# P1 of the second layer by a second Strassen level, the next batch's scores in the fixed banks, w_out in column halves, and fills into open banks

## The chip, the cores and the metric

The kernel runs on one core of a Trainium2 chip. The metric is the device time of one execution in microseconds (us). Five engines work side by side, each through its own queue in order: TensorE (PE), VectorE (DVE), ScalarE (ACT), GpSimd (POOL) and SyncE (SP), which issues the transfers.

## The reference

Two stages follow each other. In the first, x (8 batches, 8 heads, 512 rows, 64 columns) and a state (8, 8, 32, 64) attend to each other in both directions. In the second, the result, 8 x 544 rows of 512, goes through a layer with elu between two weight matrices of 512 x 2048 and 2048 x 512.

```python
def _attn_ref(x, state):
    scale = 1.0 / np.sqrt(D)
    a = softmax(scale * x @ state.T)          # max subtracted, sum + 1e-9
    xread = a @ state                          # 512 rows per batch and head
    a2 = softmax(scale * state @ x.T)
    sread = a2 @ x                             # 32 rows per batch and head
    return concatenate([xread, sread], axis=2)

def _moe_ref(x, w_in, w_out):
    h = x @ w_in
    g = np.where(h > 0, h, np.exp(np.minimum(h, 0)) - 1)
    return g @ w_out
```

(The softmax is abbreviated here.) All is in float32.

## The kernel before

**The order.** A planner in the kernel (`Plan`) records every operation with its engine, a cost and what it reads and writes, then orders them by a list schedule: PE takes its operations in the order of the code as far as they are ready, the other engines take the one that is due first. The kernel emits that order, so all recorded operations carry one line, 450. Banks of PSUM are handed out by the planner too: eight, of which two, numbers 6 and 7 (`fixed`), are kept for the third accumulator of the first layer's chunks once the steady state begins, and six rotate among everything else. Operations that only keep PE busy during the first 40 us (`fill`, line 1485) are put in where PE would idle and a bank is free.

**The stages.** `start()` loads the weights in blocks of 1 MB, converts them with ACT and DVE (16 blocks: the first eight are w_in, stored again to DRAM, the others w_out), and does the first layer of batches 0 and 1 without Strassen. It then does the second layer of batch 0 by one Strassen level, seven products P1 to P7 of 256 x 1024 by 1024 x 256 (`Strassen`). `ffn2(o, 1, x1)` does the rest of batch 1, and builds the second-level weights on the way (`Second.weights`). `batch(b)` for 2 to 7 is the steady state, and `states()` at the end does the 256 rows of the state reads.

**One batch of the steady state.** The first layer is four chunks (`ffn1_chunk`), each a Strassen level of seven products with two calls 128x256. They multiply the softmaxed scores `aT` by `m`, the product of the states and w_in (`make_m`, from w_half fetched back from DRAM). The elu of each quarter is done by ACT and DVE. The second layer (`ffn2`) starts with P1: sixteen calls 128x256 into one bank, copied out twice by ACT. P2, P6, P7, P5, P4 and P3 follow, each by a second Strassen level (`Second`): `sums` makes four sums on DVE, and `steps` has seven steps of four calls 128x128 into two banks in turn. Each step's result is added into `o` by DVE or, where it is the first one there, copied by ACT.

**What is woven into it.** After P1 the next batch's `scores` are taken into two of the rotating banks, and `first_m` makes the first block of m. The softmax of these scores (`softmax`, `softmax_rows`, on DVE, POOL and ACT) stands before P6's steps, with the loads of x (`load_x`), the state transposes with 16 small transfers (`move_state`) and the sums of aT on POOL (`sum_a`). `state_read` comes among P4's steps. The two stores of the batch and the 16 block loads for the batch after (`load_blocks`, into `o`) go through SP's queue.

```python
if six:
    o.sum_1()
    x1 = o.open()
    o.product(x1, o.a11, b11, True)
    A.copy(out=c12, in_=x1)
    A.copy(out=c11, in_=x1)
    second[2].sums(o.a12, s_2[1], a_sb[:, :1024])
    if nxt:
        scores(b + 1, xr)
        first_m(b + 1)
    for f in second[2].steps(c11):
        f()
```

Of the kernel before, what the change touches and what calls it, by code (L numbers as in the profile page):

```python
# [78 lines left out]
class Op:  # L79
    __slots__ = (  # L80
        "number", "engine", "cost", "emit", "deps", "opens", "closes", "port", "moved", "start",
        "end", "due", "users", "name", "instr", "shape", "rank", "rate", "turn", "nudge",
# [3 lines left out]
class Plan:  # L86
# [51 lines left out]
    def add(self, engine, cost, emit, ins, outs, port=False, moved=0, tokens=((), ()), name="", shape=None):  # L138
        op = Op()
        op.number, op.engine, op.cost, op.emit = len(self.ops), engine, cost, emit  # L140
        op.deps, op.opens, op.closes, op.port, op.moved = set(), None, [], port, moved
        op.name, op.shape, op.rank, op.rate = name, shape, None, 350e3
        op.nudge = 0.0
        pieces = []
        banks = {}
        for writes, aps in ((False, ins), (True, outs)):
            for a in aps:
                if isinstance(a, View):
                    banks[id(a.bank)] = a.bank
                else:  # L150
                    pieces.append((writes,) + self.region(a))
        for writes, names in enumerate(tokens):
            for t in names:
                self.writers.setdefault(t, [])
                self.readers.setdefault(t, [])
                pieces.append((bool(writes), t, 1))
        for writes, key, mask in pieces:
            if key is None:
                continue
            for m, o in self.writers[key]:  # L160
                if m & mask:
                    op.deps.add(o)
            if writes:
                for m, o in self.readers[key]:
                    if m & mask:
                        op.deps.add(o)
        for writes, key, mask in pieces:
            if key is None:
                continue
            if writes:  # L170
                self.writers[key] = [
                    (m & ~mask, o) for m, o in self.writers[key] if m & ~mask
                ] + [(mask, op)]
                self.readers[key] = [(m & ~mask, o) for m, o in self.readers[key] if m & ~mask]
            else:
                self.readers[key].append((mask, op))
        for b in banks.values():
            if b.last is None:
                b.first = op
            else:  # L180
                op.deps.add(b.last)
            b.last = op
        op.deps.discard(op)
        self.ops.append(op)
        return op
# [51 lines left out]
    def run(self, until=0.0):  # L237
# [13 lines left out]
        port, wire, shape = 0.0, 0.0, None  # L251
# [4 lines left out]
        def bank_time(op):  # L256
# [4 lines left out]
            if op is not openers[oldest]:  # L261
                need += self.KEPT_BANKS
# [3 lines left out]
        def choice(op):  # L266
            if op.number < self.all_banks:
                return banks
            return [b for b in banks if b[1] not in fixed]

        def pick(e):
# [4 lines left out]
            while able[e] or coming[e]:  # L276
# [4 lines left out]
                for _, n, op in able[e]:  # L281
                    start = max(at, ready[op])
                    if op.port:
                        start = max(start, port)
                    if op in self.opening or op in self.kept:
# [17 lines left out]
        while len(done) < len(self.ops):  # L303
# [8 lines left out]
            if e == PE:  # L312
                t = free_at[PE]
                while at < until and t + 0.5 < at:
                    free = [i for u, i in banks if u <= t]
                    if free:
                        fills.append((t, free[-1]))
# [12 lines left out]
            while oldest < len(openers) and openers[oldest] in opened:  # L330
                oldest += 1
            if e == PE and op.shape != shape:
# [46 lines left out]
def kernel(  # L379
# [49 lines left out]
    ident = pool.tile([P, P], FP32, name="ident")  # L429
    w_out = buffer([FO, DM], "w_out")  # L430
    t_w_sb = buffer([3, FO // 2, 256], "t_w")
    sec = buffer([9728], "sec")
    sec_2 = buffer([1536], "sec_2")
    g_sb = buffer([FO, S], "g")
    kT = buffer([B + 2, P], "kT")
# [5 lines left out]
    soft = buffer([1024], "soft")  # L441
    s_buf = buffer([2048], "s")
    xe = buffer([2048], "xe")
    small = buffer([68], "small")

    make_identity(nc, ident)

    def issue(engine, name, kw):
        def emit():
            ins = getattr(engine, name)(**{k: resolve(v) for k, v in kw.items()})  # L450
# [7 lines left out]
    class Engine:  # L458
# [3 lines left out]
        def __getattr__(self, name):  # L462
            def call(**kw):
# [11 lines left out]
                elif self.key == ACT:  # L475
                    cost = 0.055 + 0.84 * n
                    cost += 0.1 * sum(is_ap(kw[k]) for k in ("scale", "bias") if k in kw)
# [45 lines left out]
    def turn_calls(outs, in_):  # L523
# [28 lines left out]
    def tops(g):  # L552
        return dict(
            top=small[:, g : g + 1], total=small[:, 2 + g : 3 + g],
            top_t=small[:, 4 + 16 * g : 20 + 16 * g], total_t=small[:, 36 + 16 * g : 52 + 16 * g],
        )
# [84 lines left out]
    def scores(b, xT):  # L641
        st[b, "s"] = ps = [bank(), bank()]
# [10 lines left out]
    def make_m(b, *hcs):  # L653
# [10 lines left out]
        products(0.46 * len(hcs), calls, "make_m", "state")  # L664

# [39 lines left out]
    def soft_t(g):  # L705
        return soft[:, g * 512 : (g + 1) * 512]
# [5 lines left out]
    def read(b):  # L712
        return kT[:, B + b if b < 2 else b - 1]

    def softmax_rows(b):
        s = st[b, "s"]
        top, total = small[:, 0:2], small[:, 2:4]
        for g in range(G):
            V.reduce_max(out=tops(g)["top"], in_=s[g], axis=AX_X)
        V.tensor_scalar(out=top, in0=top, scalar1=-scale, scalar2=None, op0=ALU.mult)  # L720
        for g in range(G):
            A.activation(
                out=soft_a(b, g), in_=s[g], func=AF.Exp, scale=scale, bias=tops(g)["top"],
                accum_out=tops(g)["total"],
# [4 lines left out]
    def softmax(b, to):  # L729
        s = st[b, "s"]  # L730
        total_t = small[:, 36:68]

        def rows(g):
            return soft_t(g).rearrange("p (k n) -> p k n", n=NS)

        for g in range(G):
            V.transpose(out=soft_t(g), in_=s[g])
        for g in range(G):
            V.reduce_max(out=tops(g)["top_t"], in_=rows(g), axis=AX_X)
            Q.tensor_tensor(  # L740
                out=rows(g), in0=rows(g), in1=bc(tops(g)["top_t"], NS), op=ALU.subtract
            )
            A.activation(out=soft_t(g), in_=soft_t(g), func=AF.Exp, scale=scale)
            V.reduce_sum(out=tops(g)["total_t"], in_=rows(g), axis=AX_X)
        V.tensor_scalar(out=total_t, in0=total_t, scalar1=eps, scalar2=None, op0=ALU.add)
        V.reciprocal(out=total_t, in_=total_t)
        for g in range(G):
            Q.tensor_tensor(
                out=rows(g), in0=rows(g), in1=bc(tops(g)["total_t"], NS), op=ALU.mult
            )  # L750
            V.transpose(out=to[:, g * 512 : (g + 1) * 512], in_=soft_t(g))
# [23 lines left out]
    def state_read(b, at=x_halves):  # L775
# [12 lines left out]
        for g in range(G):  # L788
            A.activation(
                out=read(b)[:, g * D : (g + 1) * D], in_=ps[:, g * D : (g + 1) * D], func=AF.Copy,  # L790
                scale=tops(g)["total"],
# [52 lines left out]
    def ffn1_chunk(b, c, g_to):  # L844
# [14 lines left out]
        def part_1():  # L859
# [6 lines left out]
            elu(pa, g_to[:, k0, lo], e[0], V)  # L866
# [3 lines left out]
        def part_2():  # L870
# [6 lines left out]
            elu(pc, g_to[:, k0, hi], e[3], V)  # L877
# [10 lines left out]
    w_k = w_out.rearrange("p (k e) (h q) -> p k e h q", e=2, h=2)  # L888
    b11, b12, b21, b22 = (halves(w_k[:, :, e, h]) for e in range(2) for h in range(2))
# [8 lines left out]
    class Second:  # L898
# [23 lines left out]
        def sums(self, a, s, s34=None):  # L922
# [5 lines left out]
            s = s.rearrange("p (i k q) -> p i k q", i=2, q=P)  # L928
            s1, s2 = s[:, 0], s[:, 1]
            if s34 is None:  # L930
                s3, s4 = a21, a12
            else:
                s34 = s34.rearrange("p (i k q) -> p i k q", i=2, q=P)
                s3, s4 = s34[:, 0], s34[:, 1]
# [4 lines left out]
            if s34 is not None:  # L939
                V.tensor_tensor(out=s4, in0=a12, in1=s2, op=ALU.subtract)  # L940
            self.late = s34 is None

        def steps(self, out, fresh=False):
# [6 lines left out]
            def step(n, ps, a, b, first, last, h, c):  # L950
# [11 lines left out]
                o = out[:, h, c * P : (c + 1) * P]  # L962
                if fresh and n in (0, 2, 3, 6):
                    A.copy(out=o, in_=ps)
                else:
                    V.tensor_tensor(out=o, in0=o, in1=ps, op=ALU.add)
# [18 lines left out]
    second[2] = Second(sec_2)  # L985
    s_2 = [sec[:, 7680 + i * 1024 : 7680 + (i + 1) * 1024] for i in range(2)]
# [83 lines left out]
    def weight_block(n, parts=1):  # L1070

        out = []
        for i in range(parts):
# [5 lines left out]
            else:  # L1079
# [3 lines left out]
                dst = w_out[:, rows, q * 256 : (q + 1) * 256]  # L1083
# [6 lines left out]
    def ident_ready(i):  # L1090
        v = fixed[i].view()
# [4 lines left out]
                (v[:, k * P : (k + 1) * P], ident, ident, dict(start=k == 0, stop=True))  # L1096
# [6 lines left out]
    def start():  # L1103
# [79 lines left out]
        late = plan.ops[-1]  # L1183
        n0 = Strassen(2, g0, [m_sb[:, i, :1024] for i in range(2)], s_buf)
# [51 lines left out]
    def ffn2(o, b, x1=None):  # L1236
# [4 lines left out]
        if six:  # L1241
            o.sum_1()
            x1 = o.open()
            o.product(x1, o.a11, b11, True)
            A.copy(out=c12, in_=x1)
            A.copy(out=c11, in_=x1)
            second[2].sums(o.a12, s_2[1], a_sb[:, :1024])
            if nxt:
                scores(b + 1, xr)
                first_m(b + 1)  # L1250
            for f in second[2].steps(c11):
                f()
            second[6].sums(o.s, s_2[0], m_sb[:, 1, :1024])
            combine(o.a12, o.a12, o.s)
            if nxt:
                softmax(b + 1, a_sb)
                softmax_rows(b + 1)
                load_x(b + 1, x_halves)
                move_state(b + 1)
                sum_a()  # L1260
            steps = second[6].steps(c12)
            second[7].sums(o.a21, s_2[1])
            for f in steps:
                f()
            combine(o.s, o.s, o.a11, ALU.add)
            A.copy(out=c21, in_=c12)
        else:
# [3 lines left out]
            second[6].sums(o.s, s_2[0], m_sb[:, 1, :1024])  # L1271
# [10 lines left out]
        if not nxt:  # L1282
            turn_read()
        elif not six:
# [25 lines left out]
        if not six:  # L1310
            second[2].weights(b21)
        for f in second[3].steps(c12):
            f()
        store(b, 0, o)

    def turn_read():
# [3 lines left out]
        for b in range(B):  # L1320
            calls += turn_calls(
                [v[t][:, b] for t in range(2)], read(b)
# [9 lines left out]
    def batch(b):  # L1332
        for hc in range(4, 7):
            fetch(hc)
        if b + 1 < B:
            load_blocks(b + 1, ob)
        p = [None] * FC
# [24 lines left out]
    def state_chunk(c, right):  # L1362
# [15 lines left out]
        spare = (soft, a_sb)[c % 2]  # L1378
# [104 lines left out]
    def fill(i):  # L1483
        tc.keep_in_program_order(
            nc.tensor.matmul(
                psum[:, i, :P], ident, ident, start=True, stop=True, skip_group_check=True
# [4 lines left out]
    for op in steps:  # L1491
        while fills and fills[0][0] <= op.start:
            fill(fills.pop(0)[1])
# [32 lines left out]
```

## Time and profile before

| what | value |
|---|---|
| median of 3 runs | 710.66 us (710.53 to 711.33) |
| the profiled execution | 709.55 us, its span 707.8 us |
| PE busy | 694.1 us, 98% |
| DVE busy | 561.3 us, 79% |
| ACT busy | 292.5 us, 41% |
| POOL busy | 123.5 us, 17% |
| one batch of the steady state | about 76.4 us (250.75 to 327.07, and so on) |
| mean granted PE clock | 0.995 |

The span is the time from the first to the last instruction; the execution's own time has some 1.75 us more around it. Busy time is the union of an engine's instructions. A call of a float32 matmul shows as two records, whose durations overlap those of their neighbours. The chain of waits is followed back from the last instruction: at each step to what released it. In the timeline a line shows start, length, engine, operation and, in brackets, the idle time before it and what ended it. In the table by stretches the columns are the length of the stretch, then busy time and instructions of PE, its weight loads, DVE, ACT and POOL, the granted clock, the share of the transfer engines and GB/s.

### The profile page before, as it was taken

To read this page: it belongs to the slowest core of one execution; us is meant where nothing else is said; L and a number is where in the kernel's file an instruction comes from. 1 tells how busy PE (TensorE), PEld (TensorE's weight loads), DVE (VectorE), ACT (ScalarE), POOL (GpSimd) and SP (SyncE) were. 2 spreads that over 40 slices of the span, in tenths; PEclk is the share of its full clock that TensorE was granted. 3 is DMA by queue.
4 is the path that set the end of the run, shared out by engine and by line. 5 is a ranking of instruction groups with operands and counts; after the bars stand their busy time and mean duration, and the time that the engine had idled before them with its cause. 6 is when DMAs were issued, how large, how long until landed. Compare 5 with 4: busy or idle time off the path is not lost.

```text
span 707.8 us, 14536 instructions
## 1 busy us (share of the span) xinstructions
PE 694.1 (98%) x5792; PEld 592.0 (84%) x5792; DVE 561.3 (79%) x1049; ACT 292.5 (41%) x575; POOL 123.5 (17%) x158
## 2 busy tenths in 40 slices
PE   8799999999999999999999999999999999999997
PEld 7444467889988999889978998899988998999996
DVE  3988999999749984899569974998589955998650
ACT  3979972011147312741075214721284107410530
POOL 1300000023111232120430241123212033000000
PEclk9999999999999999999999999999999999999999
DMA  9578774223263424442373316242444223200300
GB/s 219 185 235 279 253 242 77 61 42 108 61 146 109 116 80 117 123 119 36 99 195 65 86 60 159 96 117 79 125 115 121 49 100 122 61 1 31 119 8 24
DMA packets 132772, 78.55 MB, mean 111 GB/s; under 512 B 113760, under 2 KB 114272, under 8 KB 132704
## 3 DMA queue, kind: packets, MB, share of 16 engines
q1 hardware_dynamic: 130492, 77.06, 39.1%
q8 instruction: 46, 0.75, 0.4%
q10 hardware_dynamic: 2212, 0.56, 0.4%
q14 instruction: 22, 0.18, 0.1%
HBM read 61.34 MB, written 13.11 MB: 105 GB/s over the span
## 4 chain that ended last, share of the span: by engine, by line
PE 94%; ACT 2%; DVE 2%; DMA 1%; issue 0%; POOL 0%; ACTq 0%; DVEq 0%
PE ps L450 93%; DMA xe<-in_x_dram 1%; ACT o L450 1%; DVE w_out L450 1%; ACT w_half L450 0%; ACT t_w L450 0%; DVE s L450 0%; ACT sec L450 0%; POOL soft L450 0%; DVE t_w L450 0%; ACT soft L450 0%; ACTq L450 0%; ACT s L450 0%; DVE g L450 0%; DVE soft L450 0%
## 5 line engine op out<-in xcount | busy, mean ns | idle before, releaser
L450 PE MATMUL ps<-aT,m 128*128 128x256 f32 (+1 forms) x568 | 149.4, 409 | 0.3 <-ACT m L450 0.3
L450 PE MATMUL ps<-w_out,g 128*128 128x128 f32 (+1 forms) x864 | 143.2, 314 | 0.0
L450 PEld LDWEIGHTS ps<-w_out,g 128*128 128x128 f32 x864 | 126.3, 191 | 10.4 <-issue 2.1
L450 PEld LDWEIGHTS ps<-aT,m 128*128 128x128 f32 x568 | 106.1, 191 | 33.1 <-issue 15.2
L450 DVE TENSOR_TENSOR o<-o,ps 128x128 f32<-128x128 f32 (+2 forms) x263 | 73.7, 288 | 53.1 <-PE ps L450 52.4
L450 POOL TENSOR_TENSOR m<-m 128x256 f32<-128x256 f32 x72 | 54.5, 774 | 245.7 <-ACT m L450 244.7
L450 PE MATMUL ps<-sec 128*128 128x128 f32 x560 | 74.7, 276 | 1.8 <-ACT o L450 1.8
L450 PEld LDWEIGHTS ps<-sec 128*128 128x128 f32 x560 | 68.1, 192 | 3.2 <-ACT o L450 2.7
L450 ACT COPY o<-ps 128x128 f32<-128x128 f32 (+2 forms) x54 | 20.5, 406 | 111.8 <-PE ps L450 102.5
L450 PE MATMUL ps<-t_w,s 128*128 128x128 f32 (+1 forms) x432 | 66.1, 300 | 0.0
L450 PEld LDWEIGHTS ps<-t_w,s 128*128 128x128 f32 x432 | 58.9, 191 | 5.7 <-DVE o L450 2.1
L450 ACT ACTIVATE xe<-ps 128x512 f32<-128x512 f32 x96 | 53.6, 600 | 14.1 <-DVE ps L450 8.7
L450 POOL TENSOR_TENSOR soft<-soft,small 128x512 f32<-128x512 f32 x32 | 33.4, 1063 | 147.3 <-DVE small L450 147.3
L450 ACT COPY ps<-ps 128x512 f32<-128x512 f32 (+1 forms) x28 | 15.2, 544 | 102.3 <-PE ps L450 102.0
L450 ACT COPY m<-ps 128x512 f32<-128x512 f32 (+1 forms) x56 | 27.4, 542 | 65.2 <-PE ps L450 65.2
L450 DVE TENSOR_TENSOR ps<-sec,ps 128x512 f32<-128x512 f32 x48 | 32.6, 689 | 15.0 <-PE ps L450 11.8
L450 PE MATMUL ps<-aT,s 128*128 128x256 f32 x168 | 41.0, 379 | 0.0
L450 PE MATMUL ps<-w_half,kT 64*32 64x256 f32 x1024 | 36.1, 389 | 1.9 <-DVE w_half L450 1.9
L450 ACT COPY sec<-ps 128x512 f32<-128x512 f32 x48 | 28.3, 589 | 20.5 <-PE ps L450 20.5
L450 PEld LDWEIGHTS ps<-aT,s 128*128 128x128 f32 x168 | 31.9, 190 | 4.3
L450 DVE TENSOR_TENSOR g<-g 128x512 f32<-128x512 f32 (+1 forms) x37 | 32.9, 890 | 0.1
L450 DVE TENSOR_TENSOR g<-xe,ps 128x512 f32<-128x512 f32 x48 | 32.3, 685 | 0.8
(145 smaller groups left out, 1134.5 us busy)
## 6 DMA issues: line engine op xcount, KB each, us to landing
w_half<-w_in_mem SPq DMA_DIRECT2D x54, 512.0 KB
t_w<-in_moe_w_out_dram SPq DMA_DIRECT2D x8, 1024.0 KB
t_w<-in_moe_w_in_dram SPq DMA_DIRECT2D x7, 1024.0 KB
out_dram<-o SPq DMA_DIRECT2D x14, 512.0 KB
xe<-in_x_dram SPq DMA_DIRECT2D x26, 256.0 KB
o<-in_x_dram SPq DMA_DIRECT2D x80, 64.0 KB
w_in_mem<-w_half SPq DMA_DIRECT2D x8, 512.0 KB
xr<-xr SPq DMA_DIRECT2D x96, 32.0 KB
```

The costliest lines, as they stand in the source:

```text
L450: ins = getattr(engine, name)(**{k: resolve(v) for k, v in kw.items()})
```

## The change

P1 of batches 2 to 7 becomes a second-level product like the other six: a new `second[1]` with its own weights (`sec_1`), its four sums, and seven steps of four calls into c12. The two 128x512 copies fall away; P2's first additions read c12 and write c11 (`base`). After P1's first step stands `first_m`, then the scores, which now go into the two fixed banks. The softmax and what hangs on it stand behind P7's sums. To make room in SBUF, the early softmax buffer, the identity and the small values of batches 0 and 1 move into `sec_1` before its weights are made, and the later softmax works in `xr`. A second identity is made on POOL for the last batch, where `turn_read` comes earlier.

w_out is stored as two column halves, each contiguous, instead of rows of 512. Three of the elus of each batch (of chunk 2 one, of chunk 3 two) take their second pass on ACT instead of DVE. In the planner POOL waits when an operation of DVE [...] would be due first (`give_way`). Where no bank is free, a fill goes into a bank that is open, adding zeros into columns not yet used (`spare`).

```diff
-    w_out = buffer([FO, DM], "w_out")
+    w_out = buffer([2, FO, DM // 2], "w_out")
+    sec_1 = buffer([1536], "sec_1")
...
+        def give_way(op, start):
+            waits = [
+                max(free_at[DVE], t) for t, _, o in coming[DVE] if o.port and o.due < op.due
+            ]
...
+            first = min(waits, default=math.inf)
+            return start if first > start + op.cost else max(start, first + 0.01)
...
                     if free:
-                        fills.append((t, free[-1]))
+                        fills.append((t, free[-1], 0))
+                    elif spare:
+                        fills.append((t, spare.index, 1))
...
-    def scores(b, xT):
-        st[b, "s"] = ps = [bank(), bank()]
+    def scores(b, xT, at=None):
+        st[b, "s"] = ps = at or [bank(), bank()]
...
-            elu(pa, g_to[:, k0, lo], e[0], V)
+            elu(pa, g_to[:, k0, lo], e[0], A if c == 3 else V)
...
-            elu(pc, g_to[:, k0, hi], e[3], V)
+            elu(pc, g_to[:, k0, hi], e[3], A if c > 1 else V)
...
-                o = out[:, h, c * P : (c + 1) * P]
-                if fresh and n in (0, 2, 3, 6):
+                o, p = (x[:, h, c * P : (c + 1) * P] for x in (out, base or out))
+                if n not in (0, 2, 3, 6):
+                    p = o
+                elif fresh:
+                    p = None
+                if p is None:
                     A.copy(out=o, in_=ps)
                 else:
-                    V.tensor_tensor(out=o, in0=o, in1=ps, op=ALU.add)
+                    V.tensor_tensor(out=o, in0=p, in1=ps, op=ALU.add)
...
         if six:
             o.sum_1()
-            x1 = o.open()
-            o.product(x1, o.a11, b11, True)
-            A.copy(out=c12, in_=x1)
-            A.copy(out=c11, in_=x1)
-            second[2].sums(o.a12, s_2[1], a_sb[:, :1024])
+            second[1].sums(o.a11, spaces(m_sb[:, 1], 3) + s_2[0][:1])
+            steps = second[1].steps(c12, fresh=True)
+            steps[0]()
             if nxt:
-                scores(b + 1, xr)
                 first_m(b + 1)
-            for f in second[2].steps(c11):
+                scores(b + 1, xr, [f.view() for f in fixed])
+            else:
+                turn_read()
+            for f in steps[1:]:
                 f()
-            second[6].sums(o.s, s_2[0], m_sb[:, 1, :1024])
+            second[2].sums(o.a12, s_2[1] + spaces(a_sb))
+            for f in second[2].steps(c11, base=c12):
+                f()
+            second[6].sums(o.s, s_2[0] + spaces(m_sb[:, 1]))
             combine(o.a12, o.a12, o.s)
-            if nxt:
-                softmax(b + 1, a_sb)
...
             second[7].sums(o.a21, s_2[1])
+            late = plan.ops[-1]
             for f in steps:
                 f()
             combine(o.s, o.s, o.a11, ALU.add)
             A.copy(out=c21, in_=c12)
+            if nxt:
+                with plan.behind(late):
+                    softmax(b + 1, a_sb)
+                    softmax_rows(b + 1)
+                    load_x(b + 1, x_halves)
+                    move_state(b + 1)
+                    sum_a()
...
             second[2].weights(b21)
+            second[1].weights(b11)
...
+    def fill(i, part):
+        rhs = zeros.to_broadcast([P, P]) if part else ident
         tc.keep_in_program_order(
             nc.tensor.matmul(
-                psum[:, i, :P], ident, ident, start=True, stop=True, skip_group_check=True
+                psum[:, i, part * 256 : part * 256 + P], ident, rhs, start=not part, stop=True,
+                skip_group_check=True,
             )
         )
```

## The prediction

> **What bounds the kernel now.** I read the page's busy shares first, then its chain of waits, then both in time.
>
> ```profile
> PE 694.1 (98%) x5792; PEld 592.0 (84%) x5792; DVE 561.3 (79%) x1049; ACT 292.5 (41%) x575; POOL 123.5 (17%) x158
> ...
> PE 94%; ACT 2%; DVE 2%; DMA 1%; issue 0%; POOL 0%; ACTq 0%; DVEq 0%
> ```
>
> TensorE (PE) is busy for 98% of the span and is 94% of the chain that ended last. The chain in order of time says where the other 6% lie: before 35 us, between 99 and 109 us (VectorE converting the last of w_out), at the end, and five times some 0.33 us on ACT and in handovers, one per batch from 2 to 6. Between them PE runs 76 us without a break:
>
> ```profile
> 34.97 64.67 PE ps L450 x400
> ...
> 251.08 76.00 PE ps L450 x688
> ```
>
> So in the steady state a change is worth what it takes from, or adds to, PE's own queue, plus any new wait. How long a product occupies PE must be read from start to start in PE's timeline, because the listed durations overlap:
>
> ```profile
> 275.96 1.89 PE L450 MATMUL ps<-aT,m 128*128 128x256 f32 x8
> 277.78 1.09 PE L450 MATMUL ps<-w_half,kT 64*32 64x256 f32 x32
> 278.80 8.90 PE L450 MATMUL ps<-aT,m 128*128 128x256 f32 x40
> ...
> 304.30 5.34 PE L450 MATMUL ps<-w_out,g 128*128 128x256 f32 x24
> 309.58 1.09 PE L450 MATMUL ps<-xr,kT 64*32 64x512 f32 x16
> 310.46 1.07 PE L450 MATMUL ps<-w_half,kT 64*32 64x256 f32 x32
> 311.46 2.05 PE L450 MATMUL ps<-w_out,g 128*128 128x128 f32 x16
> 313.35 1.06 PE L450 MATMUL ps<-t_w,s 128*128 128x128 f32 x8
> 314.24 1.06 PE L450 MATMUL ps<-sec,sec 128*128 128x128 f32 x8
> ...
> 326.00 1.06 PE L450 MATMUL ps<-sec 128*128 128x128 f32 x8
> 327.41 1.16 PE L450 MATMUL ps<-sec 128*128 128x128 f32 x8 [0.35 <-ACT o L450]
> ```
>
> One call is two records. 313.35 to 314.24 is 0.893 us for four calls 128 wide, so 0.2233 us a call. Eight records 256 wide take 1.73 us (300.85 to 302.58 in the same answer), so 0.4325 us a call. A call of half the width costs 0.516 of the whole, not 0.5. The last line is the 0.35 us wait: two steps in a row into one bank, the second waiting until ScalarE (ACT) has copied the first out.
>
> The start shows a second limit, in the clock column of the table by stretches:
>
> ```profile
> 28.00:30.00 2.00, 1.31 (x4) 0.24 (x2) 2.00 (x4) 2.00 (x6) 0.04 (x1) 1.00 0.85 337
> 30.00:32.00 2.00, 0.66 (x4) 0.42 (x4) 2.00 (x4) 2.00 (x7) 0.00 (x0) 0.98 0.00 0
> 32.00:34.00 2.00, 1.23 (x24) 0.68 (x32) 2.00 (x5) 2.00 (x3) 0.19 (x1) 0.50 0.14 13
> ...
> 38.00:40.00 2.00, 2.00 (x5) 0.83 (x4) 2.00 (x3) 0.74 (x2) 0.00 (x0) 0.81 0.54 217
> ```
>
> After PE idles 0.91 us (to 30.22) and 1.90 us (30.87 to 32.77), its clock is 0.50 from 31.9 to 38.75 us. At 34.97 PE becomes the chain, so 3.78 us of it run at half rate: 1.89 us lost.
>
> [...] records 128 wide last 276 ns on average but follow every 112 ns. [...] This bears on the planner's new give_way, but POOL is idle 83% of the span, and VectorE's durations beside it (0.70 us for a transpose) equal those without, so I price it at nothing.
>
> **The change, part by part.**
>
> *P1 of batches 2 to 7.* The built order has 96 calls 128x256 fewer and 168 calls 128x128 more. Per batch: 16 x 0.4325 = 6.92 us become 28 x 0.2233 = 6.25 us. Six batches: **-4.0 us**, all on PE.
>
> *VectorE and ACT for it.* Per batch four sums 128x512, priced at 0.60 us start to start (2.4), and three adds 128x128 (0.2 each, 0.6), less three tensor_scalar that moved to ACT (0.33 each, 1.0): +2.0 us on VectorE. ACT gets three 128x512 passes (0.6 each) and four 128x128 copies (0.27) for two 128x512 copies (0.59): +1.7 us. ACT is busy 30 of 76 us per batch, so that hides. VectorE is the doubtful cover: in batch 3 it is busy 38.5 of 39.0 us from 298 to 337, then 9.1 of 15.3. But the softmax (12 operations of 0.6 us and small ones, about 8 us) moves behind P7's sums, out of the full stretch, while the sums come in. The third step of P1 needs two sums that follow the last first-layer product by about 3.9 us (five VectorE operations and two ACT passes at 0.6, with handovers), and PE has 4.8 us of other work queued there (four steps and the scores). Hidden, with 0.9 us to spare.
>
> *Scores apart from make_m.* Before, scores and the first make_m stand together: from 309.58 to 311.46, with 0.09 and 0.10 at the joints, 2.07 us. In the new order they stand apart. A lone make_m costs 1.20 (1.02 plus two joints, 277.78), lone scores 1.21 (141.06 to 142.08, plus joints): 2.41. Batches 2 to 6: 5 x 0.34 = **+1.7 us**.
>
> *The 0.35 us wait.* P7's two steps into one bank have another step between them in the new order of every batch: **-1.75 us**, if ACT copies promptly. ACT now has softmax passes of 0.64 us in that queue; in the worst case as much comes back, so 0 to -1.75, and I take all.
>
> *Softmax and state moves later.* Behind the two state transposes SP issues 16 DMAs (10.9 us here at 318.94), then the two stores and the next block loads. state_read waits for these DMAs, and the rest of PE's queue waits for state_read. From those transposes to state_read the order has 17 steps and one short product, 16.1 us; DMAs and landing need about 10.9 + 2.2 (landing estimated from the 2.0 us between the last block issue's end at 364.2 and the transpose at 366.1) = 13.1. Spare 3 us: price 0. The block loads start about 1.2 us later in the batch; VectorE stood 5.6 us waiting for them at 358.38 with PE running on, and the first add behind that wait starts as late as before: 0. The w_half fetches go ahead of the state moves, once make_m frees the slots four steps earlier: 0.
>
> *Fills.* Seven more, all in the gap from 30.87 us: 7 x 0.2233 = 1.56 us of 1.90, so they delay nothing. [...] If the clock holds, PE gains up to 1.89 us by 38.75; VectorE and ACT were themselves waiting for PE there (2.4 and 2.3 us idle between 37 and 45), so the later conversions move with it. I take **-1.6**, bounds 0 and -1.9.
>
> *The rest.* w_out in halves: 0.015 us less on each of 16 VectorE operations, 0.25 us where VectorE holds PE at 108.92: 0 to -0.25, and -1.3 if that wait closes; I take 0. t-weights of b11 (four VectorE sums, 2.8 us, in batch 1, where VectorE idles 15 us), one more restore, a copy for read(1), an identity on idle POOL, turn_read earlier: hidden.
>
> Sum: -4.0 + 1.7 - 1.75 - 1.6 = -5.65. The profiled execution took 709.55 us (span 707.8 and 1.75 around it), 1.1 below the median 710.66. Own time 703.9, median **705.0**.
>
> **Rivals.**
> *A, VectorE returns it:* in its full stretch it misses PE by 0.3 to 0.8 us per batch, 5 or 6 times, 2 to 4 us: 707 to 709. For it: 38.5 of 39 busy and 0.9 us spare. Against: PE stood only 0.35 us per batch with the same load.
> *B, the clock falls anyway* [...]: 1.6 back, 706.6.
> *C, slower:* state_read waits for the state moves. PE is in order, so each microsecond that the 16 DMAs are late is five in the end. It decides from 3 us (eaten slack) plus 5.65/5 = 1.1 us: landing 4.1 us later than worked out. At 5.5 us late: 5 x 2.5 - 5.65 = +6.9, 717.5. For it: w_half fetches of 512 KB share the engines then. Against: the issue queue sets the 10.9 us.
> *D:* the new order does not do what it says: excluded for P1 by the call counts.
>
> **How the numbers follow.** Forecast 0.60, A 0.17, B 0.12, C 0.09, neither 0.02. What a measurement can tell from no change is about 0.2%, 1.4 us. Faster holds the forecast, B and nearly all of A: 0.86; same 0.05, slower 0.09. Range: below, the full clock gain and a closed wait at 108.92 (another 1.6) and something over, 703.0; above, A with its 4 us, 709.2.
>
> **What would show it.** PE's spacing in P1 at 0.893 per step; w_half and xr,kT apart; no 0.35 us wait; batches near 75.6 us (76.35 - 0.67 + 0.34 - 0.35 = 75.67); clock 1.00 from 32 to 39 us. Wrong, if PE waits for DVE m, sec or o within 300 to 340, for DMA xr at state_read, or the clock column still shows 0.50.

## The result, and the profile after

The changed kernel takes **722.62 us** (median of 4 runs, 721.80 to 722.91), the kernel before 710.60 (4 runs): a ratio of 1.0172 with a 95% interval of 1.0149 to 1.0196. Forecast was 705.0. The profiled execution took 722.37 us. First the busy line and the chain by engine, from the page of after (the same lines of before stand at the head of the prediction):

```profile
PE 700.1 (97%) x5950; PEld 595.9 (83%) x5950; DVE 595.2 (83%) x1078; ACT 301.3 (42%) x606; POOL 145.7 (20%) x161
...
PE 56%; DVE 34%; issue 4%; ACT 3%; DMA 2%; SPq 1%; POOL 0%; DVEq 0%; ACTq 0%; POOLq 0%
```

Before, VectorE was 2% of the chain that ended last; now it is 34%. VectorE has 29 instructions more and 33.9 us more busy time, more than twice the 14.8 that six batches with 2.0 more each (the prediction's count) and four weight sums (2.8) would give. POOL has 3 instructions more and 22.2 us more. So operations that were there already have become longer. Two names for what follows: the program's buffers lie in SBUF, and `ps` in the lines is PSUM, to which every line of PE in the two pages writes. Groups of VectorE from 175 us (before, first fence) and 180 us (after, second fence) to the end of the batches, kept apart by shape; the figure after the bar is busy time, then the mean of one in ns:

```profile
L450 DVE TENSOR_TENSOR ps<-sec,ps 128x512 f32<-128x512 f32 x48 | 32.6, 689 | 15.0 <-PE ps L450 11.8 <-ACT sec L450 1.8 <-DVE g L450 0.5
L450 DVE TENSOR_TENSOR sec<-g 128x512 f32<-128x512 f32 x23 | 16.2, 703 | 0.0
L450 DVE TENSOR_TENSOR g<-g,sec 128x512 f32<-128x512 f32 x17 | 11.7, 685 | 0.0
```

```profile
L471 DVE TENSOR_TENSOR ps<-sec,ps 128x512 f32<-128x512 f32 x48 | 33.1, 689 | 9.2 <-PE ps L471 4.1 <-ACT sec L471 4.0
L471 DVE TENSOR_TENSOR sec<-g 128x512 f32<-128x512 f32 x21 | 18.4, 874 | 0.0
L471 DVE TENSOR_TENSOR g<-g,sec 128x512 f32<-128x512 f32 x17 | 15.3, 900 | 0.0
```

A sum with one input in PSUM still takes 689 ns; these two groups of sums with both inputs in SBUF went from about 690 to 870-900. Other such groups rose less (`sec<-sec,g` from 693 to 782) or not at all (`s<-s,sec`, 677), so it depends on what runs beside them. What they meet is seen in the timeline of after, all engines, in batch 3 (start, length, engine, operation; in brackets the idle time before and its end):

```profile
342.88 2.31 POOL L471 TENSOR_TENSOR aT<-aT 128x256 f32<-128x256 f32 x2
...
344.73 1.01 DVE L471 TENSOR_TENSOR o<-o 128x512 f32<-128x512 f32 x1
...
345.15 2.31 POOL L471 TENSOR_TENSOR m<-m 128x256 f32<-128x256 f32 x2
...
346.80 0.27 DVE L471 TENSOR_TENSOR o<-o,ps 128x128 f32<-128x128 f32 x1
346.99 1.01 DVE L471 TENSOR_TENSOR g<-g 128x512 f32<-128x512 f32 x1
...
347.12 0.38 PE L471 MATMUL ps<-sec 128*128 128x128 f32 x1 [0.21 <-DVE o L471]
```

Beside POOL's sums of aT and m each of VectorE's five sums from 343.59 to 349.14 takes 1.01 us, and two of POOL's 2.31 (before, at 340.28, three took 2.09, with adds from PSUM beside them). PE does not wait for a sum but for the short add (0.27) that empties a bank and stands behind it in VectorE's queue. There is a second such place, in P1:

```profile
312.26 1.21 DVE L471 TENSOR_TENSOR sec<-g 128x512 f32<-128x512 f32 x1
313.02 1.06 PE L471 MATMUL ps<-sec,m 128*128 128x128 f32 x8
313.39 1.21 DVE L471 TENSOR_TENSOR sec<-g,m 128x512 f32<-128x512 f32 x1
...
314.53 0.27 DVE L471 TENSOR_TENSOR o<-o,ps 128x128 f32<-128x128 f32 x1
...
314.85 0.38 PE L471 MATMUL ps<-w_out,m 128*128 128x128 f32 x1 [0.78 <-DVE o L471]
```

There POOL runs the sums of m after first_m (309.86, four in 4.20 us). PE waits for DVE o 20 times, 8.6 us in all; before there was no such wait of PE. The loss is larger than this idle time, because listed matmuls overlap (a step lasts 1.06 us and the next follows after 0.893): in batch 3 six steps start late behind such an add, by 2.7 us together from start to start, and the waits list 1.4 us of it. From state_read in batch 2's second layer to the one in batch 6's are four batches: 279.04 to 593.62, 78.65 us each, against 76.36 before. Batch 1's second layer, too, has four such waits, of 0.42 to 0.94 us, and ends 3.6 us later against its own start.

The start went better than forecast. A line of the table by stretches of after (columns as above; the granted clock is the third from the end):

```profile
32.00:34.00 2.00, 1.57 (x37) 0.78 (x35) 2.00 (x5) 1.71 (x3) 0.12 (x1) 1.00 0.12 25
```

The clock is 1.00, where it was 0.50 before, and PE's 1.34 us wait for VectorE at 108.92 is gone: batch 2's scores start at 138.38 instead of 141.06.

### The profile page after: what moved, and what is told of

Read it like the earlier page. It is cut to its first block, busy times and chain, and to the rows that moved or that the text cites. A ratio compares the mean times of both kernels' runs of the same rounds, so it can differ in the third digit from the quotient of the medians.

```text
span 720.4 us, 14910 instructions
## 1 busy us (share of the span) xinstructions
PE 700.1 (97%) x5950; PEld 595.9 (83%) x5950; DVE 595.2 (83%) x1078; ACT 301.3 (42%) x606; POOL 145.7 (20%) x161
## 4 chain that ended last, share of the span: by engine, by line
PE 56%; DVE 34%; issue 4%; ACT 3%; DMA 2%; SPq 1%; POOL 0%; DVEq 0%; ACTq 0%; POOLq 0%
PE ps L471 55%; DVE sec L471 8%; DVE g L471 7%; DVE o L471 5%; DVE small L471 4%; DVE s L471 3%; DVE m L471 2%; DVE xr L471 2%; DMA w_in_mem<-w_half 1%; ACT xe L471 1%; DVE aT L471 1%; PE ps L1534 1%; DVE ps L471 1%; SPq L471 1%; ACT xr L471 1%
## 5 line engine op out<-in xcount | busy, mean ns | idle before, releaser
L471 PE MATMUL ps<-w_out,g 128*128 128x128 f32 (+1 forms) x768 | 113.3, 294 | 1.9 <-DVE o L471 1.2
L471 PEld LDWEIGHTS ps<-w_out,g 128*128 128x128 f32 x768 | 102.3, 191 | 12.4 <-DVE o L471 2.4
L471 POOL TENSOR_TENSOR m<-m 128x256 f32<-128x256 f32 x72 | 65.3, 925 | 111.1 <-ACT m L471 110.1
L471 POOL TENSOR_TENSOR xr<-xr,small 128x512 f32<-128x512 f32 x24 | 30.1, 1272 | 225.6 <-DVE small L471 130.7
L471 ACT ACTIVATE xe<-ps 128x512 f32<-128x512 f32 x96 | 55.5, 600 | 9.0 <-DVE ps L471 6.6
L471 DVE SCALAR_TENSOR_TENSOR g<-xe,ps 128x512 f32<-128x512 f32 x66 | 44.0, 681 | 11.0 <-ACT xe L471 10.7
L471 DVE TENSOR_TENSOR ps<-sec,ps 128x512 f32<-128x512 f32 (+1 forms) x52 | 34.8, 669 | 9.3 <-PE ps L471 4.1
L471 ACT ACTIVATE xe<-xe 128x512 f32<-128x512 f32 x66 | 40.6, 638 | 0.9
L471 PE MATMUL ps<-sec,g 128*128 128x128 f32 (+1 forms) x300 | 37.5, 272 | 0.2
L471 ACT COPY sec<-ps 128x512 f32<-128x512 f32 (+1 forms) x52 | 29.6, 569 | 18.5 <-PE ps L471 15.5
```

The costliest lines, as they stand in the source:

```text
L471: ins = getattr(engine, name)(**named)
```

## The experiments

Theories: **PORT** (a label only: no view shows a port), POOL's operations and VectorE's sums with two SBUF inputs lengthen each other, as in the lines above (1.01 us for a sum instead of 0.68, 2.31 for two of POOL's where three took 2.09), and the change makes them coincide. **LOAD**, VectorE's 2 us more per batch are too much by themselves. **SOFTMAX/PLACE**, the later softmax crowds them. **GIVE**, give_way causes the coincidence. **FIXED**, the scores in banks that nobody waits for cause it. **ORDER**, it is POOL's work as such and the planner's order of it.

| kernel | median us | ratio to before (95%) | us per batch |
|---|---|---|---|
| e1_thin_pool | 704.71 | 0.9911 (0.9876-0.9947) | 76.08 |
| e2_plain_p1 | 726.95 | 1.0220 (1.0187-1.0252) | 79.98 |
| e3_startup | 706.57 | 0.9950 (0.9929-0.9972) | 76.37 |
| c_before_thin_pool | 712.10 | 1.0013 (0.9988-1.0038) | 76.27 |
| e4_soft_early | 724.53 | 1.0199 (1.0180-1.0218) | 79.59 |
| e5_no_give | 732.98 | 1.0319 (1.0284-1.0353) | 81.40 |
| e6_thin_first | 716.92 | 1.0094 (1.0071-1.0117) | 77.87 |
| e7_elu_dve | 725.88 | 1.0217 (1.0198-1.0236) | 79.39 |
| e8_start_give | 714.63 | 1.0060 (1.0037-1.0083) | 77.78 |
| e9_start_fixed | 706.28 | 0.9937 (0.9917-0.9958) | 76.95 |
| e10_start_s2 | 739.72 | 1.0431 (1.0366-1.0495) | 82.89 |
| e11_rot_banks | 731.41 | 1.0302 (1.0278-1.0327) | 80.87 |
| e12_gated | 710.81 | 0.9997 (0.9981-1.0013) | 76.83 |
| e13_gated_no_give | 714.27 | 1.0041 (1.0026-1.0057) | 77.13 |
| e14_gated_elu | 718.72 | 1.0109 (1.0081-1.0137) | 76.95 |
| e15_gated_thin_soft | 705.57 | 0.9897 (0.9873-0.9921) | 76.19 |
| e16_gated_b11 | 711.50 | 0.9994 (0.9974-1.0013) | 76.91 |

The last column is taken as above, from state_read to state_read over four batches. The kernel before, run again beside each group of experiments, had medians from 710.7 to 712.2, so a difference of 1 or 2 us between rows of different groups says little.

**Is it POOL?** In e1 (on the changed kernel) and the control (on the kernel before) POOL's sums and its two parts of the softmax are cut to a few columns, so most of that work is left out; a Relu stands for the exponential on ACT. The plan is the same.

```diff
+ if self.key == POOL and "steady" in st and name == "tensor_tensor":
+     less = {k: v[:, :2] if is_ap(v) else v for k, v in kw.items()}
- issue(self.engine, name, kw)
+ issue(self.engine, name, less)
```

> The changed kernel with every tensor_tensor of POOL from batch 1's second layer on cut to its first two columns (so the sums of m and aT and the softmax's subtraction and product are left out, and the softmax's exponential is replaced by a scaled Relu so that the numbers stay finite); order and waits are the same. Theory PORT [...]: VectorE's 128x512 sums go back from 0.8-0.9 to 0.69 us, the new waits of PE for DVE o (about 3 us per batch) fall below 0.5, batches near 75.7 us, total 705 to 708. Theory LOAD (2 us more of VectorE work per batch are too much by themselves): no less VectorE work, so 719 to 723.

> Control: the kernel before with POOL's tensor_tensor cut to two columns in the same way (same parts left out). PORT: VectorE is not what PE waits for there, so at most -1 us (709.6 to 710.6), though VectorE's sums that met POOL shrink a little. If it gains 3 us or more, POOL's results were a bound of their own[...].

e1: 704.71, all of the loss gone, 0.3 below PORT's range, though its batches (76.08) are longer than the 75.7 expected. VectorE, with the same 1078 instructions, is busy for 574.2 us instead of 595.2: 21.0 us were stretching. The same groups in e1:

```profile
L473 DVE TENSOR_TENSOR sec<-g 128x512 f32<-128x512 f32 x23 | 15.7, 684 | 0.0
...
L473 DVE TENSOR_TENSOR g<-g,sec 128x512 f32<-128x512 f32 x17 | 11.7, 688 | 0.0
```

The control gains nothing (batches 76.27 against 76.36), so POOL's work was no bound there. Both kernels also clear two buffers on POOL at the start, where PE waits 2.6 to 2.7 us for POOL instead of 1.4. Could e1 gain because POOL's results come earlier, and not because sums are no longer stretched? The waits of after speak against it: no operation of VectorE waits for POOL, PE does once, at the start, and ACT, apart from the start, three times for 1.9 us in all. LOAD falls as the main cause: e1 has all of VectorE's added work.

**Which part of the change?** P1 back at one level:

```diff
- second[1].sums(o.a11, spaces(m_sb[:, 1], 3) + s_2[0][:1])
- steps = second[1].steps(c12, fresh=True)
- steps[0]()
+ x1 = o.open()
+ o.product(x1, o.a11, b11, True)
+ A.copy(out=c12, in_=x1)
+ A.copy(out=c11, in_=x1)
```

> The changed kernel with P1 of batches 2 to 7 as before (sixteen calls 128x256, two ACT copies; no second-level weights, sums or steps for it); softmax late, scores in the fixed banks, fills and halves stay. PORT and LOAD: P1's sums are what is crowded, waits shrink to under 1 us per batch: 705 + 4 (PE's share) = 709 to 712. Theory SOFTMAX (it is the later softmax that crowds VectorE and POOL during P5 and P4): the waits at P5 and P4 stay, 716 to 722.

726.95: slower still, and slower than any theory had it, PORT's 709 to 712 included. Without the second-level P1 the sums still meet POOL (`sec<-g` at 959 ns), and PE waits for DVE o 21 times, 16.1 us. So the second-level P1 is not what costs; with the rest of the change in place it saves 4 us. Next the softmax where it stood, and give_way left out:

```diff
- with plan.behind(late):          # e4: the block moves ahead of P6's steps
-     softmax(b + 1, a_sb)
...
- if e == POOL:                    # e5
-     start = give_way(op, start)
```

> The changed kernel with softmax, softmax_rows, load_x, move_state and sum_a back where they stood before (ahead of P6's steps, no wait behind P7's sums); second-level P1, scores in the fixed banks, elus, fills, halves and give_way stay. Theory PLACE (the softmax's transposes and maxima[...] used to stand beside POOL's sums of m; moved away, sums of VectorE stand there, and at P5 and P4 all of POOL's work meets VectorE's sums): PE's waits for DVE o fall below 1 us per batch, batches 75.5 to 76.7, total 705 to 711. Theory LOAD or P1 (the second-level P1 crowds VectorE wherever the softmax is): 717 or more.

> The changed kernel without give_way in the planner (POOL's operations are ordered and timed in the plan as before). Theory PLACE: give_way acts in the plan alone and nothing on the chip makes POOL wait, so the same crowding in another order: 719 to 726. Theory GIVE (the orders that give_way makes cause the coincidence): 705 to 713.

PLACE falls: 724.53. VectorE still takes the transposes of the scores behind the sums of P1 and P2 (320.64, where it had been 312.05 before), and POOL's block from 337 to 347 us is as in after. e5 is worse, in another way, and outside the ranges of both theories: fewer sums are stretched (g<-g,sec is back at 683 ns, sec<-g has 817), but PE stops in four places for nearly 4 us for sums that VectorE has behind the softmax's transposes (before the stop below, three sums of 0.85, 1.21 and 1.21 us, so stretched as well):

```profile
344.49 2.07 PE L469 MATMUL ps<-sec 128*128 128x128 f32 x8 [3.95 <-DVE sec L469]
```

e6 cuts only the sums of m after first_m; e7 puts the elus' second pass back:

```diff
+ st["steady"] = True              # e6, with the cut of e1
  sum_m(m_to[0])
+ del st["steady"]
...
- elu(pc, g_to[:, k0, hi], e[3], A if c > 1 else V)
+ elu(pc, g_to[:, k0, hi], e[3], V)
```

> The changed kernel in which only the sums of m after first_m (four operations of POOL per batch, beside P1) are cut to two columns (this part of the computation is left out); order and waits are the same. PORT with two clusters: the waits in P1 (about 1.1 us per batch, and what batch 1 lost there) go, those at P5 and P4 stay: 713 to 718, batches about 77.5. If the first cluster starts the second: 705 to 709. If the sums of m don't matter: 721 to 723.

> The changed kernel with the second pass of the three elus back on VectorE as before. Theory PLACE: 1 us more VectorE work per batch, so the same or up to 6 us more, 721 to 729. Theory ELU (VectorE loses its time waiting for ACT's second passes, 22 us in the trace of after): 710 to 717.

e6: 716.92, so four POOL operations per batch cost 5.7 us over the whole kernel; the rest must lie elsewhere, as at P5 and P4. e7: 725.88, no faster; the move of the elus is no cause.

**The parts on the kernel before.** e3 takes only the fills and the halves; e8 adds give_way to it, e9 the order and banks of the scores, e10 the second-level P1 with its buffers:

```diff
+ if e == POOL:                                              # e8
+     start = give_way(op, start)
...
- scores(b + 1, xr)                                          # e9
- first_m(b + 1)
+ first_m(b + 1)
+ scores(b + 1, xr, [f.view() for f in fixed])
```

> The kernel before with only the fills into open banks and w_out in column halves. As forecast for the clock alone: -1.6 (709.0). As the trace of after has it (clock, and the 1.34 us wait at 108.92 closed): -2.7 (707.9), batches unchanged at 76.35.

> The kernel of e3_startup (before, with the fills and the halves) with give_way in its planner and nothing else. Theory GIVE (in the plan POOL steps aside, so VectorE's sums are put where POOL in fact runs): sums stretched above 0.75 us, batches above 77, total 709 to 716. Theory FIXED (it needs the scores in banks that nobody waits for, so that the softmax may be late): batches 76.4, total 706 to 708.

> The kernel of e3_startup with first_m ahead of the scores and the scores in the two fixed banks, no give_way, P1 by one level, softmax where it was. Theory FIXED: the softmax's transposes move behind the sums of P2 and P6, PE waits for VectorE again, batches above 77.5, total 711 to 720. Theory GIVE: 706 to 709 (scores apart from make_m costs 0.34 per batch: 708).

> The changed kernel without give_way, with the scores ahead of first_m in rotating banks, softmax where it was, elus on VectorE: that is e3_startup with only the second-level P1 (and its buffers). If the step for PE was right and VectorE holds: 706.6 - 4.0 = 702 to 704, batches 75.7. If 2 us more of VectorE per batch are too much in any order (theory LOAD): 709 or more, PE waiting for DVE sums.

e3: 706.57, scores of batch 2 at 138.10, 2.96 us earlier than before, and batches as before. e9: 706.28, as e3 in total, though its batches take 0.6 us more: FIXED falls. **e8: 714.63, 8 us more by give_way alone**, with stretched sums (this group took 0.69 at 333.80 before):

```profile
L469 DVE TENSOR_TENSOR s<-s,sec 128x512 f32<-128x512 f32 x5 | 6.1, 1212 | 0.0
```

The code gives a reason: give_way delays POOL's start in the plan only. On the chip POOL starts when its data are there (in after the sums of m start at 309.86, 0.08 us after ACT's copy of m ends at 309.78), while the order of VectorE's queue was made in the belief that POOL stands still. This is read from the code and the traces, not tried apart. In the kernel before, VectorE has operations with one SBUF input at most beside POOL's m for most of its time (to 316.10; only at the very start does a sum of `s`, 312.69 to 313.35, overlap it):

```profile
312.82 3.28 POOL L450 TENSOR_TENSOR m<-m 128x256 f32<-128x256 f32 x4 [19.93 <-ACT m L450]
...
313.45 0.72 DVE L450 STREAM_TRANSPOSE soft<-ps 128x512 f32<-128x512 f32 x1
314.08 0.26 DVE L450 TENSOR_TENSOR o<-o,ps 128x128 f32<-128x128 f32 x1
314.25 0.69 DVE L450 TENSOR_REDUCE small<-ps 128x1 f32<-128x512 f32 x1
...
315.05 0.69 DVE L450 TENSOR_REDUCE small<-ps 128x1 f32<-128x512 f32 x1
```

e10 shows that the second-level P1 without the other edits is far worse, 739.72; PE waits for DVE sec, g and o, 21.4 us in 15 waits. LOAD expected this of e10, but its sums are stretched too (o<-o 904 ns, s<-s,sec 992) and its mean clock is 0.986, so how much of it is load is open. e11 goes the other way, the changed kernel with the scores in rotating banks:

```diff
- first_m(b + 1)
- scores(b + 1, xr, [f.view() for f in fixed])
+ scores(b + 1, xr)
+ first_m(b + 1)
```

> The changed kernel with the scores ahead of first_m and in rotating banks, softmax where it was; second-level P1, give_way and elus on ACT stay. Theory FIXED: 703 to 708. Theory GIVE: the sums of VectorE stay stretched, 714 to 724.

731.41. In the timeline of e11, P1 stops right after its first step, five times for 1.4 us, and what came last is an elu's pass on ACT:

```profile
309.95 2.26 PE L471 MATMUL ps<-w_out,g 128*128 128x128 f32 x16 [1.41 <-ACT xe L471]
```

This is above the ranges of both FIXED and GIVE. It differs from e4 in the order and the banks of the scores alone, and is 6.9 us slower: the two together help the second-level P1, and by e9 they cost nothing in total without it.

**POOL's work kept, its time moved.** In e12 POOL makes the twelve sums of m and aT in one go behind a small operation that reads one of P3's sums: a wait on the chip, not in the plan. e13 leaves give_way out of it, e14 also has the elus on VectorE:

```diff
  copy_m(b + 1, 1, m_to[1])
- sum_m(m_to[1])
+ w = s_2[0][1]
+ Q.tensor_tensor(out=small_2[:, 68:70], in0=w[:, :2], in1=w[:, 2:4], op=ALU.add)
+ with plan.behind(plan.ops[-1]):
+     sum_m(m_to[0])      # gone from first_m
+     sum_a()             # gone from the softmax's block
+     sum_m(m_to[1])
```

> The changed kernel in which POOL's sums of m and aT for the next batch (12 operations) stand after a small operation of POOL that reads the second of P3's sums: a real wait on the chip, at the end of VectorE's run of sums. Nothing is left out. Theory PORT: the first cluster of waits goes as in e6_thin_first (-5.7), and of the second what the sums of aT and m make of it: 706 to 713, batches 76 to 77.3, VectorE's sums back below 0.72. Theory ORDER: 719 to 730, since POOL's work is the same and comes later.

> The kernel of e12_gated without give_way in the planner. PORT: nothing left for give_way to do but the softmax's four operations: within 3 us of e12_gated. ORDER: as e5_no_give, 728 to 738.

> The kernel of e13_gated_no_give with the second pass of the three elus back on VectorE. VectorE then has 1 us more work per batch and fewer waits for ACT: within 3 us of e13_gated_no_give if VectorE keeps up, 3 to 6 us more if it is full.

e12: 710.81, 11.8 us less than the changed kernel with all of POOL's work done. The sums also stand later in the code; the move and the wait were not tried apart. Two groups of e12:

```profile
L471 DVE TENSOR_TENSOR g<-g,sec 128x512 f32<-128x512 f32 x17 | 15.8, 926 | 0.0
L471 DVE TENSOR_TENSOR sec<-sec,g 128x512 f32<-128x512 f32 x23 | 15.7, 681 | 0.0
```

Most sums are back (o<-o is at 760); g<-g,sec is the group beside the softmax's subtraction (at 400.57 to 403.07 in e12, the sum at 400.95 taking 1.22). e13 is 3.5 us slower, a little more than the 3 us expected, and far from ORDER's 728: ORDER falls. e14 is 4.4 us slower still, as was expected of a VectorE that is full, but its four batches are no longer than e13's. In the profiled executions (718.41 and 710.59) 4.0 us lie before the scores of batch 2 (143.53 instead of 139.50, another order of the start), 2.1 more by batch 2's state_read, and 2.5 after batch 6's. So in the steady batches VectorE bears 1 us more once POOL is out of its way. Last, the softmax's operations cut in e12, and b11's weights moved to batch 2:

```diff
+ if b > 1: st["thin"] = True       # e15, in softmax, with the cut of e1
...
- second[1].weights(b11)            # e16, at the end of batch 1
+ if b == 2:                        # in batch(b), ahead of chunk 2
+     second[1].weights(b11)
```

> The kernel of e12_gated with the softmax's subtraction and product on POOL cut to two columns from batch 2 on (left out; its exponential is replaced by a scaled Relu so that the numbers stay finite). PORT: batches from 76.8 to 75.3-75.8, total 703 to 706, as e1_thin_pool. If the rest comes from the waits for ACT and loads in the first layer and not from the softmax: 709 to 711.

> The kernel of e12_gated with the second-level weights of b11 made in batch 2 instead of at the end of batch 1. If they are what batch 1 still loses against e3_startup (184.2 there would be 181.2 at state_read): -2, 708 to 709.5. If VectorE takes them early in any case because the planner fills its idle time: 710 to 712.

e15: 705.57, where e1 was, with batches of 76.19 (75.3 to 75.8 were expected): the remainder is the softmax. e16: no change.

Faster than both kernels are e3 (706.57) and e9 (706.28), which have the changes of the start without give_way and the second-level P1.

## Why the prediction was wrong

**The step that failed is the price of nothing for VectorE's operations beside POOL's.** In the trace of after, sums with two SBUF inputs go from 0.68 to 1.01 and 1.21 us beside POOL, and a transpose beside POOL's sum of m (340.83, 1.18 us) still takes 0.70 (341.35). The prediction tested it with just such a transpose, and with POOL's share of busy time, an average that says nothing of when. Its own sign of being wrong, PE waiting for DVE o between 300 and 340 us, came at 314.85. The price is 722.6 - 704.7 = 17.9 us, by e1: 5.7 by the sums after first_m (e6), 6.1 more by the other sums of m and aT (e12), and 5.2 by the softmax (e15, run in another group than e12; against the kernel before of each group it is 7); 0.9 is the difference of the two ways.

**P1 on PE, -4.0.** The spacing was as forecast, 0.893 us a step (315.85 to 316.74). But even with POOL cut, batches are 76.08 on average against 76.37 in e3, where the prediction had -0.68. Two of its four batches took 75.3, better than the 75.67 of the prediction, and have no wait of PE; the other two took 76.3 and 77.4 and wait in the first layer, 0.22 and 1.24 us, for VectorE's sums into PSUM (DVE ps). The step on PE held; that nothing else would take its place did not. That e1's total lies so near the forecast is partly luck: the start gave more than priced (2.7 us in after for 1.6), and each batch took 0.4 us more than the 75.67 worked out.

**VectorE "hidden, with 0.9 us to spare".** Worked out for the third step and its two sums, with 0.6 us from sum to sum. The step was indeed hidden: the second of these sums was through at 312.34 and the step started at 313.02. The next two sums, beside POOL, took 2.3 us from start to the end of the second (312.26 to 314.60), and what came late was the add behind them, which empties the bank for the fourth step (314.85). As a load alone the 2 us are nearly hidden (e1).

**Scores apart, +1.7:** in after a scores block holds PE for 1.02 us with 0.98 and 1.00 at the steps beside it, so the 1.21 of the prediction; held. **The 0.35 us wait:** no such wait of PE for ACT o is in after; held. **Softmax later, price 0:** held for what was asked (state_read did not wait for the state moves, rival C did not come), but not for POOL's part of the softmax. **Fills, -1.6:** the clock held: between 30 and 32 us PE is busy for 1.75 us in after, where it was 0.66, and the clock is 1.00 in each stretch from 28 to 42 us. How much idle time it bears was not tried. With the wait at 108.92 closed the start gave 2.7 us in after and 3.0 in e3; the prediction had this at the far end of its range. Which of the fills and the halves closed the wait was not tried apart.

**Rivals.** A was the right place and direction (VectorE misses PE by a few tenths, several times a batch) with a size of 2 to 4 us instead of 18, since it had VectorE's count of work and not its stretching. No rival let an operation that was already there become longer.

Open: why a second-level P1 without give_way loses more than with it (e5, e10) was read from single waits, not tried; the sums stretched there and the lower clock (0.986 in both) have a part in it that is not known. In e12 the wait and the later place of POOL's sums were not tried apart.

## What to carry to other kernels

Where VectorE and GpSimd run side by side, list which operations have both inputs in SBUF and look at what runs beside them, in time (here 0.68 us became 1.01 or 1.21); test an interference with the kind of operation whose time is in question, since here a transpose showed none of it (0.70). A rule in the scheduler that let POOL step aside in the plan did not make it step aside on the chip: give_way alone cost 8 us, and POOL's sums moved behind a real wait on a two-column operation gave 11.8. The add that emptied a bank stood behind two sums of 2.3 us together in VectorE's queue (314.53), and PE stood for 0.78 us, so the slack of the bank counts, too.

## What the runs showed of the hardware that was not expected

- The price of POOL beside VectorE: sums of 128x512 with two SBUF inputs went from 0.68 to 1.01 us beside POOL's 128x256 sums (343.59 to 349.14 in after) and to 1.21 or 1.22 beside those of m in P1 (312.26) or the softmax's 128x512 (400.95 in e12); POOL's own means went from 762 to 910 ns (m), 727 to 988 (aT) and 1047 to 1233 (softmax). Beside POOL's work in after, too, a transpose took 0.70 (341.35), an operation with one input in PSUM 0.67 (`g<-xe,ps`, 311.06) and the short adds from PSUM 0.27 (344.53). From 343.59 on, a sum and a short add of VectorE and an operation of POOL recur every 1.14 us (to 344.73; three of POOL's in 3.44). In before, with POOL idle, the next sum behind a sum and such an add starts after 0.80 (333.00 to 333.80), and three POOL operations with no sum beside them took 2.09 (340.28). Not every sum beside POOL is longer: the one at 342.77, which started ahead of POOL's operation (342.88), took 0.70, and the one at 311.66 took 0.68.
- A VectorE operation of two columns, with one tensor input and a constant, took longer as well: `small` plus a constant took 0.15 us with POOL idle (e2, 332.70), 0.56 beside the softmax's product in after (338.65) and 1.01 beside it in e12 (408.89).
- The wait of PE of 3.95 us in e5 that ends at 344.49 cost more than its length: PE at half clock follows it, and the first step behind it took 2.07 us, against 1.06 in after at 342.47. The table by stretches shows:

```profile
340.00:344.00 4.00, 0.54 (x5) 0.35 (x4) 3.97 (x6) 0.00 (x0) 3.89 (x5) 0.83 0.10 16
344.00:348.00 4.00, 3.51 (x16) 3.51 (x17) 2.73 (x6) 0.00 (x0) 0.00 (x0) 0.50 0.30 50
```

  The mean clock of e5 was 0.986 against 0.999 in after, and part of its loss is this.
